# A recurrence and a gated unit on one core: small convolution tiles, a state carried in place in PSUM, and a new loop order

The kernel runs on one core of one Trainium2 chip. The metric is device time in microseconds (us) of that core, lower is better. A run is called slow when it lies over 1.5% above the fastest of its kernel, and ratios use fast runs alone.

## What is computed

```python
# r, k, v: (4, 8, 768, 48); w, u: (8, 48); all float32
for t in range(S):                                   # a state of 48x48 per head
    cur = einsum('bhd,bhe->bhde', u * k[t], v[t])
    y[t] = einsum('bhd,bhde->bhe', r[t], state + cur)
    state = w * state + einsum('bhd,bhe->bhde', k[t], v[t])
x = y.transpose(0, 2, 1, 3).reshape(B, S, 384)
gate = sigmoid(causal depthwise convolution of x, 5 taps)
out = (gate * (x @ w_val)) @ w_out                   # both weights 384x384
```

## The kernel before

The sequence is cut into chunks of 128 positions. Inside a chunk the outputs are masked attention; between chunks a state is carried and decayed. Two chunks make a step (256 positions), so there are 12 steps, three to a batch. Each engine gets its instructions in the order of lists of tokens such as `A:0.1` (attention of the second chunk of a step). Four steps are ordered token by token in a head; eight follow in a loop, over a list called STEP.

The parts that the change touches:

```python
def bonus(n):                                  # u*k*r sums, S
    kv_ps = ps_kv.tile([128, 512], F32)        # the one state bank; step 0: another bank
    st["kv_tile", n, 0] = kv_ps                # state(n, 0) goes into the same bank
    ...                                        # 8 matmuls
def state(n, cl): ...                          # KV: 4 matmuls into kv_ps
def carry(n, cl):                              # ID: adds the decayed state, on TensorE
    nc.tensor.matmul(out=kv_ps, lhsT=ident, rhs=zin, start=False, stop=True)
def decay(n, cl):                              # ZE, on VectorE
    nc.vector.tensor_tensor(out=z, in0=kv_ps, in1=wcm, op=ALU.mult)
def y_out(n, cl):                              # Y: 40 matmuls into 32-row groups:
    ...                                        # 12 for the state, 16 attention, 12 bonus
def conv(n):                                   # C: 64x64 tiles, 4 at once
    g_ps = [ps_mm.tile([128, W + C], F32) for i in range(2)]     # 2 banks of 384 columns
    for T0, t1, tn in [(0, 0, W), (2, 0, 0)]:
        for t in range(KW):
            for q in range(2):
                for i in range(2): ...         # 40 matmuls, 20 of 256 and 20 of 128 columns
LOADS = "r0 k0 r1 k1 v0 r2 k2 Wv v1 Wo r3 v2 k3 r4 ..."          # cut; Wo ahead of r3
STEP = """
    Y:-1.1 YE:-1.1 Y:-1.0 A:0.1 A:0.0 YE:-1.0 CV:0.0 M:0.3 KS:1.0 M:0.2 S:0.0 C:-1.0 V:-1.1
    SG:-1.1 V:-1.0 SE:0.0 RS:1.0 SG:-1.0 M:0.0 DV:0.0 M:0.1 KT:1.0 RT:1.0 HT:-1.1 KV:0.0
    ID:0.0 HT:-1.0 O:-1.0 O:-1.1 ZE:0.0 KV:0.1 KE:1.0 ID:0.1 RE:1.0 ZE:0.1 OE:-1.0 OE:-1.1
    PR:1.0
"""
# A attention, M mask, S bonus, C convolution, SG sigmoid, V value, HT gate*value, O project,
# KT/RT transposes of k and r, KE/RE/YE/OE evacuations, PR product k*r, KS/RS scalings
```

Of the kernel before, what the change touches and what calls it, by code (L numbers as in the profile page):

```python
# [8 lines left out]
F32 = mybir.dt.float32  # L9
# [7 lines left out]
def kernel(  # L17
# [165 lines left out]

    wv_st = consts.tile([128, NT, DM], F32)
    wo_st = consts.tile([128, NT, DM], F32)

    wval = consts.tile([128, NT, 4, 128], BF16)
    wout = consts.tile([128, 4, DM], BF16)
    cw5b = consts.tile([KW, DM], BF16)
    cwT = consts.tile([128, NT, KW], F32)  # L190
    cwd = consts.tile([128, NT, KW, 64], BF16)
    id64 = consts.tile([128, 64], BF16)

    def prep_conv():
        nc.vector.tensor_copy(cw5b, cw5)
        cw_ps = ps_tr.tile([128, NT, 8], BF16, name="tr_ps")
        for T in range(NT):
            nc.tensor.transpose(
                cw_ps[:, T, 0:KW], cw5b[:, T * 128 : T * 128 + 128], ident[0:KW, 0:KW]
            )  # L200
        nc.vector.tensor_copy(cwT, cw_ps[:, :, 0:KW])
        for q in range(2):
            rows = slice(64 * q, 64 * q + 64)
            nc.vector.tensor_copy(id64[rows], ident[rows, rows])
        nc.vector.tensor_tensor(
            out=cwd.rearrange("p t k x -> p (t k) x"),
            in0=id64[:, None, :].to_broadcast([128, NT * KW, 64]),
            in1=cwT.rearrange("p t k -> p (t k)")[:, :, None].to_broadcast([128, NT * KW, 64]),
            op=ALU.mult,
        )  # L210

    def cast_wval():
        wv = wv_st.rearrange("p k (t x) -> p k t x", x=128)
        nc.gpsimd.tensor_copy(wval[:, :, 0::2, :], wv[:, :, 0::2, :])
        nc.gpsimd.tensor_copy(wval[:, :, 1::2, 64:128], wv[:, :, 1:3, 0:64])
        nc.gpsimd.tensor_copy(wval[:, :, 1::2, 0:64], wv[:, :, 1:3, 64:128])

    def cast_wout(part):
        if part:
            nc.scalar.copy(out=wout[64:128, 1::2, :], in_=wo_st[0:64, 1:3, :])  # L220
            nc.scalar.copy(out=wout[0:64, 1::2, :], in_=wo_st[64:128, 1:3, :])
        else:
            nc.gpsimd.tensor_copy(wout[:, 0::2, :], wo_st[:, 0::2, :])
# [83 lines left out]
    def bonus(n):  # L307
        if n == 0:
            kv_ps = ps_mm.tile([128, 512], F32, name="mm_ps")
        else:  # L310
            kv_ps = ps_kv.tile([128, 512], F32, name="kv_ps")
            st["kv_tile", n, 0] = kv_ps
        s_ps = kv_ps[:, DM : DM + U * H].rearrange("p (c h) -> p c h", c=U)
        pr = st["pr", n]
        for cl in range(U):
            for p in range(NP):
                nc.tensor.matmul(  # L317
                    out=s_ps[:, cl, 2 * p : 2 * p + 2],
                    lhsT=pr[:, p, cl * C : cl * C + C],
                    rhs=uw2[:, p, :],  # L320
                    start=(cl == 0 and p == 0),
                    stop=(cl == U - 1 and p == NP - 1),
                    skip_group_check=True,
                )
        st["s_ps", n] = s_ps
# [41 lines left out]
    def state(n, cl, idle=0):  # L367
# [7 lines left out]
        for p in range(NP):  # L375
# [5 lines left out]
                stop=(c == 0 and p == NP - 1),  # L381
# [4 lines left out]
    def carry(n, cl):  # L386
        nc.tensor.matmul(  # L387
            out=st["kv_ps", n, cl].rearrange("p n a d -> p (n a d)"),
            lhsT=ident,
            rhs=st["zin", n, cl].rearrange("p n a d -> p (n a d)"),  # L390
            start=False,
            stop=True,
            skip_group_check=True,
        )
# [52 lines left out]
    def conv(n, idle=0):  # L447
        b, cu = divmod(n, NU)
        xT, t0 = xT_t[b % 2], cu * W
        g_ps = [ps_mm.tile([128, W + C], F32, name="mm_ps") for i in range(2)]  # L450
        warm(g_ps[0][:, 0:C], idle)
        parts = [(0, 0, W), (2, 0, 0)]
        if n == N - 1:
            parts = [(0, 0, C), (0, C, C), (2, 0, 0)]
        for T0, t1, tn in parts:
            for t in range(KW):
                for q in range(2):
                    for i in range(2):
                        T = 2 if T0 else i
                        c0, n0, o0 = (i * C, C, W) if T0 else (t1, tn, t1)  # L460
                        rows = slice(64 * q, 64 * q + 64)
                        qo = (q + i) % 2
                        nc.tensor.matmul(  # L463
                            out=g_ps[i][64 * qo : 64 * qo + 64, o0 : o0 + n0],
                            lhsT=cwd[rows, T, t, :],
                            rhs=xT[rows, T, t0 + c0 + t : t0 + c0 + t + n0],
                            start=(t == 0 and T0 == 0 and t1 == 0),
                            stop=(t == KW - 1),
                            skip_group_check=True,
                        )  # L470
        st["g_ps", n] = g_ps

    def gate_at(n, i):
        if ("gate", n) not in st:
            st["gate", n] = ffn.tile([128, 2, W + C], BF16, name="gate")
        nc.scalar.activation(out=st["gate", n][:, i], in_=st["g_ps", n][i], func=AF.Sigmoid)  # L476

    def value(n, i, idle=0):
        b, cu = divmod(n, NU)
        xT, t0 = xT_t[b % 2], PAD + cu * W  # L480
        v_ps = ps_at.tile([128, NP, 128], F32, name="at_ps")
        v_ps = v_ps.rearrange("p n x -> p (n x)")[:, 0 : W + C]
        warm(v_ps[:, 0:C], idle)
        for kt in range(NT):
            nc.tensor.matmul(  # L485
                out=v_ps[:, 0:W],
                lhsT=wval[:, kt, i, :],
                rhs=xT[:, kt, t0 : t0 + W],
                start=(kt == 0),
                stop=(kt == NT - 1),  # L490
                skip_group_check=True,
            )
        for kt in range(NT):
            nc.tensor.matmul(  # L494
                out=v_ps[:, W : W + C],
                lhsT=wval[:, kt, 2 + i, :],
                rhs=xT[:, kt, t0 + i * C : t0 + i * C + C],
                start=False,
                stop=(kt == NT - 1),
                skip_group_check=True,  # L500
            )
        st["v_ps", n, i] = v_ps

    def gated(n, i):
        if ("hT", n) not in st:
            st["hT", n] = ffn.tile([128, 2, W + C], BF16, name="hT")
        nc.vector.tensor_tensor(  # L507
            out=st["hT", n][:, i], in0=st["v_ps", n, i], in1=st["gate", n][:, i], op=ALU.mult
        )

    def project(n, cl, idle=0):
# [4 lines left out]
        parts = [(0, cl * C, 0), (1, cl * C, 1)]  # L516
        parts.insert(1 + cl, (cl, W, 2 + cl))
        for j, (i, c0, k) in enumerate(parts):
            nc.tensor.matmul(  # L519
                out=o_ps,  # L520
                lhsT=hT[:, i, c0 : c0 + C],
                rhs=wout[:, k, :],
                start=(j == 0),
                stop=(j == 2),
# [19 lines left out]
    def ok(n):  # L544
# [6 lines left out]
        r0 k0 r1 k1 v0 r2 k2 Wv v1 Wo r3 v2 k3 r4 k4 v3 v4 k5 r5 k6 v5 r6 v6 k7 r7 k8 v7 r8 k9 v8  # L551
# [3 lines left out]
        RS:1.0 A:0.0 A:0.1 KS:1.0 PR:0.0 RS:2.0 S:0.0 M:0.2 KT:1.0 M:0.3 M:0.0 M:0.1 KS:2.0 CV:0.0  # L555
        SE:0.0 KV:0.0~4 KE:1.0 RT:1.0 ZE:0.0 RE:1.0 WV:0.0 KV:0.1 DVD:0.0 A:1.1~9 RT:2.0 M:1.3
        ID:0.1 Y:0.1 Y:0.0 PR:1.0 RE:2.0 ZE:0.1 M:1.2 KT:2.0 A:1.0 S:1.0 YE:0.1 M:1.0 YE:0.0 C:0.0
        M:1.1 KE:2.0 PR:2.0 SE:1.0 CV:1.0 A:2.1 KV:1.0~4 SG:0.0 ID:1.0 M:2.3 ZE:1.0 V:0.1 SG:0.1
        V:0.0 KV:1.1 DV:1.0 ID:1.1 M:2.2 ZE:1.1 RS:3.0 WO:0.0 Y:1.1 YE:1.1 WP:0.0 Y:1.0 KS:3.0
        S:2.0 HT:0.1 A:2.0 YE:1.0 M:2.0 SE:2.0 RT:3.0 CV:2.0 C:1.0 HT:0.0 RE:3.0 V:1.1 KV:2.0  # L560
        SG:1.0 ID:2.0 O:0.0 DVD:2.0 SG:1.1 OE:0.0 M:2.1 ZE:2.0 V:1.0 HT:1.1 Y:2.0 YE:2.0 KT:3.0
        KE:3.0 O:0.1 Y:2.1 HT:1.0 PR:3.0 A:3.1 M:3.3 YE:2.1 OE:0.1 TL:0.0 S:3.0 M:3.2 C:2.0 SG:2.0
        A:3.0 V:2.1 M:3.0 V:2.0 SG:2.1 O:1.1 KS:4.0 M:3.1 SE:3.0 CV:3.0 HT:2.0 HT:2.1 O:1.0 OE:1.1
        OE:1.0 KT:4.0 KV:3.0 KE:4.0 RS:4.0 RT:4.0 RE:4.0 O:2.1 O:2.0 ZE:3.0 KV:3.1 ID:3.1 OE:2.1
        OE:2.0 ZE:3.1 DV:3.0 PR:4.0
    """
    STEP = """
        Y:-1.1 YE:-1.1 Y:-1.0 A:0.1 A:0.0 YE:-1.0 CV:0.0 M:0.3 KS:1.0 M:0.2 S:0.0 C:-1.0 V:-1.1
        SG:-1.1 V:-1.0 SE:0.0 RS:1.0 SG:-1.0 M:0.0 DV:0.0 M:0.1 KT:1.0 RT:1.0 HT:-1.1 KV:0.0
        ID:0.0 HT:-1.0 O:-1.0 O:-1.1 ZE:0.0 KV:0.1 KE:1.0 ID:0.1 RE:1.0 ZE:0.1 OE:-1.0 OE:-1.1  # L570
        PR:1.0
    """
    TAIL = """
        Y:11.1 Y:11.0 YE:11.1 YE:11.0 C:11.0 V:11.1 SG:11.1 HT:11.1 V:11.0 SG:11.0 HT:11.0 O:11.1
        O:11.0 OE:11.1 OE:11.0
# [7 lines left out]
    def issue():  # L583

        while loads:
            x = loads[0]
            if x == "Wv":
                nc.sync.dma_start(out=wv_st, in_=moe_w_val.rearrange("(t p) n -> p t n", p=128))
            elif x == "Wo":
                nc.sync.dma_start(out=wo_st, in_=moe_w_out.rearrange("(t p) n -> p t n", p=128))  # L590
# [118 lines left out]
```

## Time and profile before

| | before |
|---|---|
| time, median of 4 runs beside the changed kernel | 105.85 us (104.90 to 107.17) |
| profiled execution, span | 101.8 us |
| TensorE instructions, weight loads counted | 4548 |
| first bonus of the loop (starts the fifth step) | 41.45 us |
| from there to the last bonus, 7 periods | 46.55 us |
| from the last bonus to the end | 13.81 us |

The page of the kernel before gives these lines: busy time with its share and number of instructions by engine, the queue of the instruction fetch (packets, MB, share), and the shares of the chain that ended last (the work followed back from the last instruction, at each step to what released it).

```profile
PE 90.7 (89%) x2266; PEld 74.4 (73%) x2266; DVE 69.4 (68%) x136; ACT 73.4 (72%) x121; POOL 63.4 (62%) x63
...
q8 instruction: 17, 0.28, 1.1%
...
PE 57%; SPq 13%; DMA 10%; ACT 5%; DVE 5%; POOL 4%; issue 3%; ACTq 0%; POOLq 0%; DVEq 0%
```

TensorE holds the chain for 57% of the span. "issue", time in which the engine on the chain waits for nothing that the profile shows, is 3%.

### The profile page before, as it was taken

How to read it: one execution, taken by the hardware profiler on the slowest of the kernel's cores; microseconds unless marked ns; L12 is line 12 of the kernel's file. 1: busy time of each engine (PE TensorE's matmuls, PEld its weight loads, DVE VectorE, ACT ScalarE, POOL GpSimd, SP SyncE). 2: the span in 40 equal slices, each digit the busy share in tenths (PEclk: the TensorE clock that was granted, in tenths of full speed). 3: DMA queues.
4: the chain of work that ended last, by engine and by line, in shares of the span. 5: the costliest groups of instructions: out<-in, count | busy, mean ns of one | idle time of the engine just before them, and what ended most of it. 6: DMA issues, size and time to landing. Idle time of an engine off the chain costs nothing.

```text
span 101.8 us, 5137 instructions
## 1 busy us (share of the span) xinstructions
PE 90.7 (89%) x2266; PEld 74.4 (73%) x2266; DVE 69.4 (68%) x136; ACT 73.4 (72%) x121; POOL 63.4 (62%) x63
## 2 busy tenths in 40 slices
PE   4998499989698899999899999999999999978840
PEld 4696297878576787888778878889788797956710
DVE  4395867898781785985956969769488595890210
ACT  5088165999885999879579598794987958836430
POOL 7927949834847949797694894966949850050000
PEclk9999999999999999999999999999999999999999
DMA  0999999597999999979897969899897999910304
GB/s 5 215 230 226 226 239 291 134 332 129 213 229 188 203 214 222 199 183 175 170 244 139 250 126 225 177 184 261 149 216 174 357 368 361 371 65 26 135 0 155
DMA packets 67345, 20.38 MB, mean 200 GB/s; under 512 B 63478, under 2 KB 67324, under 8 KB 67324
## 3 DMA queue, kind: packets, MB, share of 16 engines
q1 hardware_dynamic: 66492, 20.07, 85.3%
q8 instruction: 17, 0.28, 1.1%
q10 hardware_dynamic: 832, 0.00, 0.5%
q14 instruction: 4, 0.03, 0.1%
HBM read 15.35 MB, written 4.72 MB: 197 GB/s over the span
## 4 chain that ended last, share of the span: by engine, by line
PE 57%; SPq 13%; DMA 10%; ACT 5%; DVE 5%; POOL 4%; issue 3%; ACTq 0%; POOLq 0%; DVEq 0%
DMA r_st<-in_r_dram 10%; PE mm_ps L463 10%; PE at_ps L519 10%; PE mm_ps L412 9%; PE at_ps L485 7%; SPq L71 7%; PE tr_ps L283 4%; PE at_ps L347 4%; PE at_ps L244 4%; SPq L590 4%; PE at_ps L494 3%; PE kv_ps L376 2%; PE kv_ps L317 2%; ACT kT L292 2%; DVE at L360 2%
## 5 line engine op out<-in xcount | busy, mean ns | idle before, releaser
L360 DVE TENSOR_TENSOR at<-at_ps,mask 128x512 bf16<-128x512 f32 x48 | 30.9, 683 | 5.4 <-PE at_ps L347 5.4
L332 POOL TENSOR_TENSOR dv<-v_st,s_sb 128x768 bf16<-128x768 f32 x10 | 14.8, 1477 | 17.4 <-DVE s_sb L329 17.4
L230 POOL TENSOR_TENSOR rs<-r_st,dr 128x768 bf16<-128x768 f32 x11 | 20.1, 1829 | 4.4 <-DMA r_st<-in_r_dram 4.3
L259 POOL TENSOR_TENSOR ks<-k_st,dk 128x768 bf16<-128x768 f32 x11 | 20.7, 1886 | 2.7 <-PE kv_ps L387 1.8
L252 ACT COPY rT<-at_ps 128x1024 bf16<-128x1024 bf16 (+1 forms) x13 | 15.9, 1234 | 3.0 <-PE at_ps L244 3.0
L399 DVE TENSOR_TENSOR z<-kv_ps,wcm 128x384 bf16<-128x384 f32 x20 | 11.1, 556 | 9.8 <-PE kv_ps L387 8.1
L292 ACT COPY kT<-tr_ps 128x1024 bf16<-128x1024 bf16 x11 | 11.2, 1015 | 5.9 <-PE tr_ps L283 5.9
L507 DVE TENSOR_TENSOR hT<-at_ps,gate 128x384 bf16<-128x384 f32 x24 | 12.3, 548 | 4.3 <-PE at_ps L494 4.3
L519 PE MATMUL at_ps<-wout,hT 128*128 128x384 bf16 x72 | 13.9, 326 | 1.5 <-DVE hT L507 1.4
L476 ACT ACTIVATE gate<-mm_ps 128x384 bf16<-128x384 f32 x24 | 10.5, 489 | 5.7 <-PE mm_ps L463 5.2
L532 ACT COPY o_sb<-at_ps 128x384 f32<-128x384 f32 x24 | 10.8, 495 | 4.0 <-PE at_ps L519 4.0
L463 PE MATMUL mm_ps<-xT,cwd 64*64 64x256 bf16 (+1 forms) x500 | 12.6, 242 | 0.9 <-ACT xT L444 0.6
L485 PE MATMUL at_ps<-xT,wval 128*128 128x256 bf16 x72 | 11.9, 274 | 0.0
L268 ACT CAST vb<-v_st 128x768 bf16<-128x768 f32 x12 | 10.3, 859 | 2.2 <-DMA v_st<-in_v_dram 2.2
L444 ACT CAST xT<-mm_ps 128x384 bf16<-128x384 f32 x24 | 11.1, 507 | 1.1 <-PE mm_ps L412 0.9
L463 PEld LDWEIGHTS <-cwd 64*64 64x64 bf16 x500 | 10.7, 106 | 1.4 <-issue 1.0
L519 PEld LDWEIGHTS <-hT 128*128 128x128 bf16 x72 | 6.6, 98 | 5.4 <-DVE hT L507 1.9
L300 DVE TENSOR_TENSOR pr<-tr_ps,rT 128x1024 bf16<-128x1024 bf16 x11 | 7.5, 683 | 4.1 <-ACT kT L292 2.1
L412 PE MATMUL mm_ps<-at,vb 128*32 128x128 bf16 x384 | 9.5, 219 | 0.0
L347 PE MATMUL at_ps<-rT,kT 48*128 48x128 bf16 x192 | 8.8, 228 | 0.5 <-ACT kT L292 0.4
L244 PE MATMUL at_ps<-ident,rs 128*128 128x128 bf16 x96 | 8.2, 235 | 0.9 <-POOL rs L230 0.9
L283 PE MATMUL tr_ps<-ident,ks 128*128 128x128 bf16 x88 | 7.1, 228 | 1.7 <-POOL ks L259 1.7
(79 smaller groups left out, 142.9 us busy)
## 6 DMA issues: line engine op xcount, KB each, us to landing
r_st<-in_r_dram SPq DMA_DIRECT2D x12, 384.0 KB, 5.2
k_st<-in_k_dram SPq DMA_DIRECT2D x24, 192.0 KB, 4.6
v_st<-in_v_dram SPq DMA_DIRECT2D x24, 192.0 KB, 4.9
out_dram<-o_sb SPq DMA_DIRECT2D x11, 384.0 KB, 5.1
wv_st<-in_moe_w_val_dram SPq DMA_DIRECT2D x1, 576.0 KB
wo_st<-in_moe_w_out_dram SPq DMA_DIRECT2D x1, 576.0 KB, 7.3
out_dram<-o_sb SPq DMA_DIRECT2D x2, 192.0 KB, 1.9
wt<-in_w_dram ACTq DMA_DIRECT2D x2, 0.8 KB, 2.5
```

Source lines behind the costliest of these rows:

```text
L230: eng.tensor_tensor(out=rs_t[n % 2][:, :, ps[0] : ps[1], :, 0:D].rearrange("p s n a d -> p (n a) s d"), in0=r_st[n][:, hs], in1=dr[:, hs], ...
L252: nc.scalar.copy(out=st["rT", n][:, ps[0] : ps[1], :].rearrange("x n (i s) -> x s n i", s=2), in_=st["r_tr", n, ps[0]],)
L259: eng.tensor_tensor(out=ks_t[n % 3][:, cs, :, :, 0:D].rearrange("p c n a d -> p c (n a) d"), in0=k_st[n][:, cs], in1=dk[:, None, :, :].to_ ...
L292: nc.scalar.copy(out=st["kT", n].rearrange("x n (c i) -> x c n i", c=U)[:, cls[0] : cls[1]], in_=tr)
L332: eng.tensor_tensor(out=dv_t[n % 2].rearrange("p c (h d) -> p (c h) d", d=D), in0=v_st[n].rearrange("p c h d -> p (c h) d"), in1=st["s", n ...
L347: nc.tensor.matmul(out=at_ps[par][:, p, :], lhsT=kT[rows, p, cs], rhs=rT[rows, p, cs], start=(p == 0), stop=(p == NP - 1), skip_group_chec ...
L360: nc.vector.tensor_tensor(out=st["at", n, cl][:, par], in0=st["at_ps", n, cl][par], in1=mask[:, None, :].to_broadcast([128, NP, 128]), op= ...
L412: nc.tensor.matmul(out=y_ps[32 * q : 32 * q + 32, T, :], lhsT=lt, rhs=rh, start=q not in first, stop=last, skip_group_check=True,)
L463: nc.tensor.matmul(out=g_ps[i][64 * qo : 64 * qo + 64, o0 : o0 + n0], lhsT=cwd[rows, T, t, :], rhs=xT[rows, T, t0 + c0 + t : t0 + c0 + t + ...
L485: nc.tensor.matmul(out=v_ps[:, 0:W], lhsT=wval[:, kt, i, :], rhs=xT[:, kt, t0 : t0 + W], start=(kt == 0), stop=(kt == NT - 1), skip_group_ ...
L507: nc.vector.tensor_tensor(out=st["hT", n][:, i], in0=st["v_ps", n, i], in1=st["gate", n][:, i], op=ALU.mult)
L519: nc.tensor.matmul(out=o_ps, lhsT=hT[:, i, c0 : c0 + C], rhs=wout[:, k, :], start=(j == 0), stop=(j == 2),)
```

## The change

The intent: take work off TensorE, which bounds the loop. The convolution goes into 32x32 tiles, twelve at once, with a third gate bank; the carry becomes an add on VectorE, in place in PSUM; and all orders (loads, head, loop, tail) were searched anew with a model of the queues. The diff, cut to its core:

```diff
+    PLACE = (lambda q: q, lambda q: q ^ 2, lambda q: q ^ 1)
     def carry(n, cl):
-        nc.tensor.matmul(out=kv_ps, lhsT=ident, rhs=zin, start=False, stop=True, ...)
+        nc.vector.tensor_tensor(out=kv_ps, in0=kv_ps, in1=st["zin", n, cl], op=ALU.add)
     def conv(n):
-        g_ps = [ps_mm.tile([128, W + C], F32, name="mm_ps") for i in range(2)]
-        ...                                        (40 matmuls in 64x64 tiles)
+        g_ps = [ps_mm.tile([128, W], F32, name="mm_ps") for T in range(2)]
+        g_ps.append(ps_at.tile([128, W], F32, name="at_ps"))
+        for t in range(KW):
+            for T in range(NT):
+                for q in range(4):
+                    rows = slice(32 * q, 32 * q + 32)
+                    o = 32 * PLACE[T](q)
+                    nc.tensor.matmul(out=g_ps[T][o : o + 32, :], lhsT=cwd[rows, T, t, :],
+                                     rhs=xT[rows, T, t0 + t : t0 + t + W], ...)
     def value(n, i):                               (6 matmuls of 256 and 6 of 128 columns)
+        ...                                        (9 of 256: two tiles, then one)
+    def load_wo(): ...                             (Wo in 7 loads, rows permuted by PLACE)
     LOADS
-        r0 k0 r1 k1 v0 r2 k2 Wv v1 Wo r3 v2 k3 r4 k4 v3 ...
+        r0 k0 k1 v0 r1 Wv r2 k2 v1 r3 v2 k3 Wo r4 v3 k4 k5 ...
     STEP
-        Y:-1.1 YE:-1.1 Y:-1.0 A:0.1 A:0.0 YE:-1.0 CV:0.0 M:0.3 KS:1.0 M:0.2 S:0.0 C:-1.0 ...
+        Y:-1.1 A:0.0 Y:-1.0 M:0.0 M:0.1 S:0.0 YE:-1.1 YE:-1.0 A:0.1 C:-1.0 V:-1.0 M:0.2 SE:0.0
+        RS:1.0 M:0.3 CV:0.0 SG:-1.1 RT:1.0 SG:-1.0 HT:-1.0 V:-1.1 SG:-1.2 KV:0.0 HT:-1.1 KT:1.0
+        O:-1.0 DV:0.0 ID:0.0 ZE:0.0 RE:1.0 O:-1.1 KE:1.0 PR:1.0 OE:-1.1 KV:0.1 ID:0.1 KS:2.0
+        OE:-1.0 ZE:0.1
     HEAD, TAIL: new orders (cut)
```

## The prediction

> **What bounds the kernel now.** I read the page's busy shares first: no engine stands out alone. Then the windows, cut where a step of the main loop begins (the first matmul of `y_out`, L412). Twelve steps of 256 positions make up the kernel; eight of them, from 39.9 us to 92.6 us, are the loop, four are a hand-ordered head. The eight take 52.7 us, 6.585 us each. Columns: window, its length, then busy time and count of PE, PE weight loads, DVE, ACT, POOL, then clock, DMA share and GB/s.
>
> ```profile
> 59.99:66.53 6.54, 6.54 (x183) 5.53 (x186) 5.20 (x10) 5.38 (x10) 5.24 (x4) 1.00 0.93 195
> 79.70:86.28 6.58, 6.58 (x182) 5.55 (x185) 5.21 (x10) 5.23 (x10) 2.72 (x2) 1.00 1.04 363
> ```
>
> PE is busy for the whole of both windows and DVE idles 1.3 us in each. A full PE could still be a waiting one, so I read the chain that ended last, in order of time (start, us, what). Between 46 and 54 us it never leaves PE:
>
> ```profile
> 46.44 1.23 PE mm_ps L412 x80
> 47.67 0.55 PE at_ps L347 x16
> 48.22 0.28 PE kv_ps L317 x8
> 55.43 0.95 PE mm_ps L463 x40
> 56.39 0.43 PE at_ps L485 x3
> 52.07 0.16 PE kv_ps L387
> 52.23 0.97 PE at_ps L519 x6
> ```
>
> So in the loop TensorE is the bound, piece after piece: y 1.23, attention 0.55, bonus 0.28, convolution 0.95, value 1.10 (0.43+0.17+0.33+0.17), two transposes 0.45 each, project 0.97, state twice 0.17, carry twice 0.16; together 6.6. The head is different. Its last wait in the timeline is this one:
>
> ```profile
> 29.43 1.83 POOL L259 TENSOR_TENSOR ks<-k_st,dk 128x768 bf16<-128x768 f32 x1 [1.82 <-PE kv_ps L387]
> 31.31 0.62 PE L283 MATMUL tr_ps<-ident,ks 128*128 128x128 bf16 x8 [0.26 <-POOL ks L259]
> 33.07 0.69 DVE L300 TENSOR_TENSOR pr<-tr_ps,rT 128x1024 bf16<-128x1024 bf16 x1 [2.09 <-ACT kT L292]
> ```
>
> The releaser shown is a matmul that this scaling does not need in that way; k of step 3 was issued from 22.0 to 25.3 us and such loads land 4.6 us later, that is up to 29.9, so I take the wait for that load. Until there the head runs at the speed of the loads (DMA share 0.92 to 1.03 in every window up to 33 us). After 33.8 us PE has hardly a gap.
>
> **What the Trainium skill says.** "TensorEngine Tiling (Array Packing)", section Key Properties: tiles work independently of each other, while a change of tiling mode drains the array. The trace agrees with both. The convolution's 0.95 us is 0.09 and five rounds of 0.11 (256 columns, a third of value's 0.33) and five of 0.056 (128 columns, an eighth of the transposes' 0.45), so its four tiles run together and issuing is not its limit. The 0.09 is the change of mode: the last of eight bonus matmuls, 0.025 us apart from 61.54, starts near 61.73, and the first convolution matmul at 61.83. "TensorE: Matmul & The Clock Gate", section Part 3 (Packing small matmuls), gives a further tile about 4 ns, so twelve tiles cost hardly more than four. "VectorE: DVE Perf Modes", sections on the perf-mode tiers and the DRAIN: tensor_tensor with a PSUM operand runs at one element a cycle, and a read of what the same engine just wrote needs a semaphore. Agreed for the first, by the groups (busy us, mean ns, then idle before):
>
> ```profile
> L360 DVE TENSOR_TENSOR at<-at_ps,mask 128x512 bf16<-128x512 f32 x48 | 30.9, 683 | 5.4 <-PE at_ps L347 5.4
> L399 DVE TENSOR_TENSOR z<-kv_ps,wcm 128x384 bf16<-128x384 f32 x20 | 11.1, 556 | 9.8 <-PE kv_ps L387 8.1
> ```
>
> No run has the second yet. "PSUM — Partial Sum Buffer", section PSUM bank collisions: two engines may not read one bank at once. So the product `pr` may not read the transposed k while ScalarE evacuates it; the 2.09 us wait above shows that order.
>
> **The change, part by part.** *Convolution.* Before: 20 matmuls of 256 columns and 20 of 128, on 4 tiles, 0.95. After: 60 of 256 on 12 of 16 tiles, 5 rounds of 0.11 us plus the drain of 0.09, 0.65: saves 0.30. *Value:* nine matmuls of 0.109 instead of six of 256 and six of 128 columns: 0.98, saves 0.12. *Carry:* 16 in all, 1.33 a step, 0.16 each: saves 0.21 a step. *Order:* the attention of one half now stands between the two y halves and the other after the bonus, so two more mode changes, 2 x 0.09 lost. TensorE's floor goes from 6.6 to about 6.6-0.30-0.12-0.21+0.18 = 6.1.
>
> *VectorE.* The adds into PSUM: 16 of 128x384 at 556 ns, 1.33 a step, 0.74. The gating product becomes one of 512 and one of 256 columns, 683 + about 415 (an estimate from the 1.0 ns a column between 384 and 512): as before. Busy goes from 5.1 to about 5.85 a step, 0.95 of a 6.1 us step. *ScalarE:* three gates of 256 columns, about 0.36 each (0.49 less 128 columns), for two of 0.49: +0.1. Both stay below the floor as sums. What decides is their order.
>
> *The new circle.* Bonus and state share the one state bank. The bonus of a step must wait for the last decay of the step before, and that decay now stands on VectorE behind the product and the add. In time from the end of that decay: bonus 0.06 to 0.28, attention to 0.58 (with drains), convolution from 0.71 (its third bank waits for a mask) to 1.30, value of two tiles to 2.04, r transposes to 2.49, r evacuation (1.32, overlapping its follower by 0.1) from 2.74, k evacuation 3.97 to 5.0, product 5.05 to 5.73, add to 6.25, wait for its own semaphore, decay to 6.87. VectorE's four masks, gating and first add and decay lead to 4.9 by themselves, so no gap is left there either. The built program has each of these waits. Two of three steps close this circle (6.8 to 6.9); the third has no second state and is bound by TensorE at about 6.45. Mean 6.7. My evacuation latencies (0.25) are rounded up, and the mean of what I could shave is 0.1, so I take 6.6 a step: the loop gains nothing, although TensorE has 0.5 us less to do.
>
> *Head.* The output weights (0.59 MB) go behind k of step 3, whose load had 11 loads of 0.39 MB and 1.18 MB of weights in front of or in it, and now has 0.59 MB less. At the 220 to 300 GB/s of that stretch, 2.0 to 2.7 us sooner. v of step 0 comes earlier too, so the work ahead of it can start sooner. I count 1.9. *Tail:* the last convolution 1.04 to 0.65, its gate chain a little longer: -0.2. Sum: 105.6 - 1.9 - 0.2 + 8 x 0.015 = 103.6.
>
> **Rivals.** *(1) TensorE stays the bound.* For it: 6.1 against 6.585, and the order was searched for. Against it: the circle. It would give 105.6 - 3.9 - 2.1 = 99.6; with some stalls 101. *(2) The circle costs its full 6.75 or more and the head gives back little,* because ScalarE and VectorE were as full as PE there (6.59 us of ACT in the 6.90 us to 39.9). It would give 105.6 + 1.3 - 0.5, about 106.5. *(3) Transfers:* the loop's loads arrive at 1.18 MB in about 6.1 us (share 0.93 of 6.54), so a 6.1 us step would meet that. But the last load is issued at 73.4 us, and its step begins at 86, so eight microseconds of lead stand between: I leave it out. *(4) Twelve tiles do not run together* and 60 pairs issue at the 15 ns of y_out (1.23/80): 0.9, no gain in the convolution, circle 7.1: 107.
>
> **Range and chances.** Between rivals 1 and 2 my sum lies in the middle, with 0.2 us a step of doubt (1.6 us) and 1.2 in the head. That is some 2 us: 101.2 to 106.6. Faster needs under 103.5, so it is near even, and I lean neither way: 0.46 faster, 0.44 same, 0.10 slower.
>
> **What would show it.** Convolution pieces of 0.6 to 0.7 us right for tiling; 0.9 wrong. DVE busy over 5.7 in a loop window, with PE under 6.3 of it, right for the circle; a chain that in the loop passes through kT, pr, kv_ps add and z, and PE waiting ahead of the bonus for z, right. PE full again at 6.1 a step: rival 1. The k scaling of step 3 starting near 27 us, right for the head; at 29 wrong. An add far from 0.56 us, or steps over 6.8, would break the sum.

## The result, and the profile after

The changed kernel takes 110.44 us (110.31 to 112.64, four runs) against 105.85. The ratio is 1.046, 95% interval 1.036 to 1.056: slower, and outside the predicted range. (A ratio is the mean time of one kernel's fast runs over that of the other's of the same rounds, so it is not quite the ratio of the medians.)

The same lines of the page, after:

```profile
PE 91.5 (84%) x2448; PEld 68.5 (63%) x2448; DVE 77.0 (71%) x153; ACT 72.7 (67%) x131; POOL 64.4 (59%) x66
...
q8 instruction: 19, 0.31, 1.2%
...
PE 30%; SPq 21%; DVE 16%; ACT 14%; issue 10%; DMA 7%; DVEq 0%; ACTq 0%
```

TensorE no longer holds the chain, as intended: 57% became 30%. But "issue" went from 3% to 10% of a longer span, over 7 us more. Cut at the bonus starts:

| us | before | after | difference | predicted |
|---|---|---|---|---|
| start to first bonus of the loop | 41.45 | 45.56 | +4.1 | -1.9 |
| 7 loop periods | 46.55 | 49.07 | +2.5 | +0.1 |
| last bonus to the end | 13.81 | 14.03 | +0.2 | -0.2 |
| span | 101.8 | 108.7 | +6.9 | |

(The profiled execution of before, 103.95 us, was faster than all four timed runs of it beside the change, so the profiles differ by more than the medians.)

**The pieces came out nearly as predicted.** These are groups of the changed kernel by shape (busy us, mean ns of one, then idle before with its releaser):

```profile
L405 DVE TENSOR_TENSOR kv_ps<-kv_ps,z 128x384 f32<-128x384 f32 x16 | 8.9, 556 | 0.8 <-PE kv_ps L393 0.8
...
L505 DVE TENSOR_TENSOR hT<-at_ps,gate 128x512 bf16<-128x512 f32 x12 | 8.2, 685 | 4.2 <-PE at_ps L491 4.1
```

The add takes 556 ns. The convolution takes 0.56 us from its first to its last start where nothing stops it, 60 matmuls, against 0.81 for 40 before; the twelve tiles do run together, as the matmuls of its first round start 3 to 4 ns apart (67.19 to 67.23 us). From its first start to the first of the next piece it is 0.76 us against 0.96, so it saves 0.20 us a step of the 0.30 predicted.

**The loop without its stops.** The chain through one undisturbed step of the changed kernel (start, us, what) is the circle of the prediction, from one bonus to the decay ahead of the next:

```profile
66.58 0.35 PE kv_ps L334 x8
...
68.02 0.76 PE at_ps L491 x6
68.78 0.46 PE at_ps L264 x8
...
69.26 1.03 ACT rT L272
...
70.43 1.02 ACT kT L312
...
72.09 0.57 DVE kv_ps L405
...
72.68 0.56 DVE z L410
```

The next bonus starts at 73.29: 6.71 us for a step with two states. The next, with one, takes 6.30. Three windows from bonus to bonus in the changed kernel, and one of the kernel before (window, its length, then busy time and count of PE, PE weight loads, DVE, ACT, POOL, then clock, DMA share, GB/s):

```profile
66.58:73.29 6.71, 6.64 (x203) 5.10 (x204) 6.24 (x13) 5.17 (x11) 4.76 (x3) 1.00 1.00 209
73.29:79.59 6.30, 6.24 (x199) 4.87 (x200) 5.73 (x11) 5.46 (x10) 4.62 (x4) 1.00 0.88 191
79.59:87.92 8.33, 6.44 (x200) 5.02 (x192) 5.44 (x12) 5.90 (x12) 5.71 (x4) 1.00 1.11 356
```

```profile
61.54:68.24 6.70, 6.70 (x192) 5.69 (x189) 5.20 (x11) 5.54 (x11) 5.09 (x4) 1.00 0.94 198
```

So an undisturbed two-state step is as long as before, 6.71 against 6.70, though TensorE's pieces are shorter. The prediction said just that. (One of its signs failed: PE was to be busy for under 6.3 us, and the profile counts 6.64 of 6.71.) The third window is what it did not say.

**The stops.** In the chain of the changed kernel, inside the window of 8.33 us:

```profile
81.06 0.65 PE at_ps L491 x5
81.71 1.42 issue
83.13 0.27 PE at_ps L491
```

Five of six value matmuls run, then TensorE stands for 1.42 us with nothing to wait for. I numbered TensorE's instructions in the order of the program, weight loads counted, and laid the trace over them. The sixth matmul is number 3775, and number 3777 is 193 above a multiple of 256. Counted from 0, every gap marked "issue" of TensorE that I followed, in every kernel of this study, lies one or two instructions ahead of such a number, 193 + 256 k. The packets of the page's q8 line, the instruction fetch, are 16 KB each (0.31 MB in 19), and there are 17 of them for the 4548 instructions of before and 19 for 4905: one for about 256 instructions. In the traces such a packet takes 0.9 to 2.1 us, and where TensorE stops it goes on 1.2 to 1.7 us after the packet's end. Over all 20 profiles, laid over their programs in the same way: of 341 crossings of such a border (449 paired with the first packet, 705 with the second, and so on) none came sooner than 1.19 us after the packet's end. So TensorE goes on only when the next block has come. What starts a packet, no record shows.

Counting gaps over 0.2 us between the starts of two matmuls at these borders, between first and last bonus of the loop: 0.76 us before (two), 2.99 us after (three, of 0.45, 0.85 and 1.69). Less its stops, a loop period is 6.54 us before and 6.58 after. So in this pair of profiles 2.2 us of the loop's 2.5 are stops.

The larger of the two stops before, at number 1984, stands in the stretch from 46 to 54 us that the prediction read as never leaving PE. Its list of lines took the convolution of the next step instead of this one:

```profile
48.51 0.90 PE mm_ps L463 x36
49.40 0.26 issue
49.66 0.25 PE mm_ps L463 x4
```

**The head.** The prediction said that the k scaling of step 3 would start near 27 us, and it does: 27.30 us, against 29.43 before.

```profile
27.30 1.81 POOL L279 TENSOR_TENSOR ks<-k_st,dk 128x768 bf16<-128x768 f32 x1 [1.66 <-DMA k_st<-in_k_dram]
```

Yet the loop starts 4.1 us later. The chain of the changed kernel there:

```profile
28.20 3.21 DMA wo_st<-in_moe_w_out_dram
...
31.51 0.13 ACT wout L241
...
32.25 0.93 ACT gate L481 x3
33.18 0.91 ACT kT L312
```

The output weights, now loaded behind k of step 3, land at 31.4 us. ScalarE, in order, waited 3.75 us for them, with three sigmoids and the k evacuation of step 3 behind. And this execution's granted clock was 0.5 to 0.7 from 32.6 to 40.8 us, right after TensorE had stood still: six project matmuls took 1.92 us there, 0.97 elsewhere. I count about 2 us for that (projects 0.95, r transposes 0.4, convolution 0.5, others 0.2).

### The profile page after: what moved, and what is told of

Same layout as the page of the kernel before. It is cut to its first block, busy times and chain, and to the rows that moved or that the text cites.

```text
span 108.7 us, 5534 instructions
## 1 busy us (share of the span) xinstructions
PE 91.5 (84%) x2448; PEld 68.5 (63%) x2448; DVE 77.0 (71%) x153; ACT 72.7 (67%) x131; POOL 64.4 (59%) x66
## 4 chain that ended last, share of the span: by engine, by line
PE 30%; SPq 21%; DVE 16%; ACT 14%; issue 10%; DMA 7%; DVEq 0%; ACTq 0%
SPq L71 14%; PE mm_ps L468 6%; ACT kT L312 6%; PE at_ps L491 5%; PE at_ps L518 5%; ACT rT L272 4%; DVE at L377 4%; PE mm_ps L423 4%; DVE kv_ps L405 4%; DVE z L410 4%; PE at_ps L364 4%; DMA r_st<-in_r_dram 4%; DVE hT L505 3%; DMA wo_st<-in_moe_w_out_dram 3%; PE at_ps L264 3%
## 5 line engine op out<-in xcount | busy, mean ns | idle before, releaser
L349 POOL TENSOR_TENSOR dv<-v_st,s_sb 128x768 bf16<-128x768 f32 x11 | 16.2, 1477 | 24.7 <-PE at_ps L468 15.5
L505 DVE TENSOR_TENSOR hT<-at_ps,gate 128x512 bf16<-128x512 f32 (+1 forms) x24 | 13.1, 553 | 9.9 <-PE at_ps L491 6.1
L518 PE MATMUL at_ps<-wout,hT 128*128 128x384 bf16 x72 | 15.0, 343 | 2.9 <-ACT wout L241 1.7
L491 PE MATMUL at_ps<-xT,wval 128*128 128x256 bf16 x108 | 15.5, 273 | 1.4 <-issue 1.4
L468 PE MATMUL mm_ps<-xT,cwd 32*32 32x256 bf16 x480 | 10.9, 283 | 1.8 <-issue 1.3
L481 ACT ACTIVATE gate<-mm_ps 128x256 bf16<-128x256 f32 x24 | 8.2, 383 | 5.3 <-PE at_ps L468 4.6
L364 PE MATMUL at_ps<-rT,kT 48*128 48x128 bf16 x192 | 10.1, 222 | 2.1 <-ACT kT L312 0.9
L468 PE MATMUL at_ps<-xT,cwd 32*32 32x256 bf16 x240 | 10.6, 283 | 0.0
L468 PEld LDWEIGHTS <-cwd 32*32 32x32 bf16 x720 | 7.4, 89 | 5.0 <-issue 3.1
L491 PEld LDWEIGHTS <-wval 128*128 128x128 bf16 x108 | 9.2, 97 | 1.9 <-issue 0.2
```

The lines of the kernel that those rows point to most:

```text
L349: eng.tensor_tensor(out=dv_t[n % 2].rearrange("p c (h d) -> p (c h) d", d=D), in0=v_st[n].rearrange("p c h d -> p (c h) d"), in1=st["s", n ...
L468: nc.tensor.matmul(out=g_ps[T][o : o + 32, :], lhsT=cwd[rows, T, t, :], rhs=xT[rows, T, t0 + t : t0 + t + W], start=(t == 0), stop=(t == K ...
L491: nc.tensor.matmul(out=v_ps[:, j], lhsT=wval[:, kt, T, :], rhs=xT[:, kt, t0 : t0 + W], start=(j == 0 and kt == 0), stop=(kt == NT - 1), sk ...
L505: nc.vector.tensor_tensor(out=st["hT", n][:, Ts], in0=st["v_ps", n, i][:, 0 : 2 - i], in1=st["gate", n][:, Ts], op=ALU.mult,)
L518: nc.tensor.matmul(out=o_ps, lhsT=hT[:, T, cl * C : cl * C + C], rhs=wout[:, T, :], start=(T == 0), stop=(T == NT - 1),)
```

## The experiments

All outputs are right. The table has what the profiles show; first bonus, stops (in the loop) and period (loop less its stops, by 7) as defined above. A profile is one execution, and the stops differ from one to the next, so times are judged by the timed runs. Profiles that fell in a slow run are marked s; I use them for the places of the stops, not for differences. Only the change, after_again, spread and both are classed as clearly slower than before; the record calls the other comparisons unclear. They ran on several chips, each beside its own runs of before. The single run before_again, beside the other runs of before on its chip (103.34 to 109.06 us), would count as slow.

| run | instructions | median us | ratio to before | first bonus | stops | period |
|---|---|---|---|---|---|---|
| before | 4548 | 105.85 | | 41.45 | 0.76 | 6.54 |
| before_again | 4548 | 107.01 (one) | | 42.27 | 3.07 | 6.53 |
| the change | 4905 | 110.44 | 1.046 | 45.56 | 2.99 | 6.58 |
| after_again | 4905 | 110.58 | 1.044 | 43.78 s | 5.71 s | 6.73 s |
| wo_early | 4905 | 109.74 | 1.044 | 44.35 | 2.75 | 6.56 |
| wo_late | 4905 | 108.21 | 1.021 | 42.06 | 2.20 | 6.59 |
| head_before | 4876 | 112.43 | 1.077 | 44.58 | 5.22 | 6.76 |
| order_before | 4883 | 118.66 | 1.134 | 45.31 | 2.93 | 7.85 |
| bonus_bank | 4907 | 113.37 | 1.086 | 42.68 | 0.40 | 7.68 |
| carry_pe | 4937 | 110.85 | 1.053 | 42.91 | 1.81 | 6.81 |
| bonus_tr | 4905 | 109.32 | 1.039 | 42.28 | 2.08 | 6.56 |
| both | 4937 | 110.59 | 1.037 | 42.46 s | 5.20 s | 6.95 s |
| shift112 | 5017 | 109.14 | 1.036 | 42.88 | 4.92 | 6.42 |
| spread | 4905 | 110.41 | 1.048 | 44.48 s | 1.43 s | 7.05 s |
| conv64 | 4185 | 108.50 | 1.031 | 42.60 | 0.32 | 7.06 |
| y_wide | 4313 | 115.72 | none given | 43.21 | none | 7.78 |
| dv_first_late | 4473 | 108.21 | none given | 43.05 | 1.31 | 6.61 |

Theory: the loop is a circle that is no shorter than before; the stops at block borders (every 256 instructions) lengthen it; ScalarE's wait for the output weights delays the head. Rivals are named in the expectations.

### Is the profile typical?

**after_again** and **before_again** are the two kernels once more.

> The changed kernel itself once more, on the chip of the next three, for its spread: 109.5 to 111.5 us, stops at instructions 1729, 2497, 3777 and 4545 again. If the dip of the granted clock around 33 to 41 us was of that one execution, it is elsewhere or gone and the first bonus of the loop comes at 42.3 to 43; if it belongs to this order of work, it is there again and the first bonus is at 45 to 46.

> The kernel before once more with a profile, for its granted clock: if the dips seen in most profiles of the changed kernels also fall on the kernel before, there is a stretch of some slices under 0.9 in this profile or none by chance; if they belong to the new order alone, none. Time 104 to 107.

The borders are the same, with 2241 added (1.66 us), and the stops are larger. The dip of the clock came at another place, and one fell on the kernel before too (0.6 and 0.5 between 10 and 18 us). So dips belong to neither order. They also do not make the difference: one timed run of the change had a granted clock of 1.000 and took 110.31 us, one of before had 1.000 and took 103.73. (The first bonus of after_again, 43.78 us, lies between the two ranges expected.) Stops are not fixed either: the kernel before had 3.07 us in its second profile, and its loop then took 48.79 us, only 0.3 less than the change's 49.07. So one pair of profiles does not settle how many microseconds of stops the change adds.

### The head

**wo_early** puts Wo back ahead of r3 in the loads.

```diff
-r0 k0 k1 v0 r1 Wv r2 k2 v1 r3 v2 k3 Wo r4 v3 k4 k5 ...
+r0 k0 k1 v0 r1 Wv r2 k2 v1 Wo r3 v2 k3 r4 v3 k4 k5 ...
```

> Changed kernel with one thing back as it was: the output weights are loaded ahead of r of step 3 again. Theory H (head): the slower head comes from ScalarE, which casts the output weights in order and sat 3.7 us on their load, with everything behind it; expected: that wait is gone, the first bonus of the loop (45.56 us in the changed kernel, 41.51 before) comes at 41 to 42, the dip of the granted clock at 33 to 41 us is gone, time 106 to 107. Rival: the head is slow because of its new order of tokens; then the first bonus stays near 45 and the time near 110.

The wait on Wo was gone, but the wait moved: GpSimd's scaling of r waited 4.8 us for its load and ScalarE's cast of v 4.7 us for its own. First bonus at 44.35, no gain, in a profile whose clock was at 0.5 from 25.6 to 32.4 us. The expectation was missed.

**head_before** takes LOADS and HEAD from the kernel before (with a third sigmoid in each step).

> The changed kernel with the orders of loads and of the head (everything ahead of the loop) as they were before, the loop's order and all other parts as changed. Head theory (the new head is what starts the loop late): the first bonus of the loop at 41.5 to 42.5 us instead of 45.6, and the time 107 to 108. Rival (the head costs what it costs because of the parts, the third gate bank and the split loads): first bonus after 43.5 and the time 109 to 110.5. The block borders fall elsewhere, which moves stops by about 1 us either way.

Missed too: first bonus at 44.58, 112.43 us. The clock was at 0.5 from 11 to 18 us, but order_before below has the same head, no such dip ahead of its loop, and 45.31. The old head does not fit the new parts, so the new head as such is not at fault. (This execution also had stops of 2.73 and 1.52 us in the loop.)

**wo_late** leaves the loads and moves the cast of Wo and the projection that needs it.

```diff
-... V:0.1 DVD:2.0 WO:0.0 C:1.0 ... V:1.0 O:0.1 KE:3.0 Y:2.0 PR:3.0 Y:2.1 YE:2.0
+... V:0.1 DVD:2.0 C:1.0 ... V:1.0 KE:3.0 Y:2.0 PR:3.0 Y:2.1 WO:0.0 O:0.1 YE:2.0
```

> The changed kernel with the cast of the output weights on ScalarE (and the one projection that needs it at once) moved later in the head, behind the evacuation of the fourth step's k; the loads and the loop are untouched. Head theory (ScalarE, held up by the output weights that land at 30 to 31.5 us because seven small loads in a row take SyncE's queue 4.5 us, delays the sigmoids and evacuations behind it): no wait on the output weights over 1 us, first bonus of the loop at 40.5 to 41.8, time 1 to 2 us under the changed kernel's. Rival (the head is bound by the loads behind, r and k of the fourth and fifth step): first bonus stays at 42.3 to 43, time unchanged.

No wait on Wo is left, and the time falls by 2.2% against after_again on the same chip (means of the two fast runs of each, 107.24 and 109.67). The first bonus, 42.06 us, just misses the 41.8 expected. From 20 us on the chain has no load in it; between 30 and 34 us, for one, it is TensorE's own work:

```profile
30.88 0.66 PE at_ps L491 x6
31.53 1.23 PE mm_ps L423 x80
32.76 0.59 PE at_ps L518 x3
```

So the wait is gone, and behind it stands the engines' own work: no kernel with the new parts started its loop before 42.06 us. How much of the 2.4 us is the head is not shown. The wait stands in the other kernels with the old place of the cast too, as in bonus_tr:

```profile
30.02 0.83 ACT L241 CAST wout<-wo_st 128x768 bf16<-128x768 f32 x1 [2.69 <-DMA wo_st<-in_moe_w_out_dram]
```

It is 1.0 us in carry_pe, 2.2 in conv64 and shift112, 2.7 in bonus_tr and 3.75 in the change, and the first bonus comes at 42.91, 42.60, 42.88, 42.28 and 45.56. In the first four the clock was full from 16 us up to the loop, and carry_pe's chain from 20 us on has no load in it either. So a wait of up to 2.7 us hardly delays the loop. Of the change's 45.56, the longer wait and the clock dip share the rest; no run separates them.

### The circle

**order_before**: the new parts, all orders as before.

> Small tiles, third gate bank and in-place carry on VectorE as changed, but loads, head, loop and tail in the order of before: the parts without the new order. If the new order is at fault: first bonus of the loop at 41.5 to 42.5 us, undisturbed steps at or under 6.6 us, and the time 103.5 to 106. If the parts themselves are at fault (VectorE's adds on the state's path, or stops at block borders, which the smaller tiles bring in any order): steps of 6.7 to 7.1 us and 107 to 110.

Periods of 7.85 us. VectorE's add stands in line ahead of other work and waits for TensorE's state, 8.2 us in the window from 45 to 100 us (waited for, times, longest):

```profile
DVE kv_ps L405 <- PE kv_ps L393: 8.2, 9, 1.0
```

The gating product stands behind the add, and TensorE's projection waited 6.3 us for that product. The new order is not the fault; without it the parts lose 1.3 us a period. (In the kernel before, VectorE's decay waited 6.1 us for the same state in the loop at no such loss, so the wait by itself is not the sign; what stands behind it is.)

**bonus_bank** and **bonus_tr** move bonus out of the state's bank, into the convolution's pool and into the bank of the k transposes:

```diff
-        kv_ps = ps_kv.tile([128, 512], F32, name="kv_ps")
-        st["kv_tile", n, 0] = kv_ps
+        kv_ps = ps_tr.tile([128, 512], F32, name="tr_ps")        # bonus_bank: ps_mm, "mm_ps"
```

> Changed kernel with the bonus in a bank of the y and gate pool, not in the state bank, so that it needs no decay of the step before. Theory C (circle): the loop's period of 6.71 us in steps with a second state is the circle bonus, convolution, value, r and k evacuation, product, add, decay; cut, undisturbed steps fall to 6.1 to 6.35 and the time by 2 to 3 us to about 108. Rival D: VectorE's own length (four masks, gating, two adds, two decays, product) sets 6.7; then the period stays above 6.6 and the time within 0.8 us of 110.4.

> The changed kernel, but the bonus sums go to the bank of the k transposes instead of the state's bank, so that bonus no longer waits for the decay of the state before; unlike bonus_bank, no other bank changes hands. Circle theory (bonus to state to add to decay to bonus sets an undisturbed step at 6.71 us): undisturbed two-state steps fall to 6.1 to 6.45 us, the wait of bonus for the decay is gone, and the time falls by 1.5 to 2.5 us to 108 to 109. Rival (VectorE's or TensorE's length sets the step): undisturbed two-state steps stay at 6.6 to 6.75 us and the time at 110 to 111.

bonus_bank tells nothing of the circle, as it made a new wait, of the convolution's bank for the bonus evacuation, in the window from 42 to 92 us:

```profile
PE mm_ps L467 <- DVE s_sb L345: 7.2, 7, 1.5
```

bonus_tr did take the wait away, with no other of TensorE in its place, and its period is 6.56. The circle through the shared bank is cut, and on average the step is not shorter: the rival, "another length sets the step", was right on that. The single steps differ: two two-state steps, less their stop, come to 6.1 and 6.2 us, as the circle theory had it, while two without a stop take 7.31 and 7.11. The time, 109.32 us, lies between the two expected. The chain of bonus_tr leads through VectorE's own queue, its masks behind its decay:

```profile
61.70 0.57 DVE kv_ps L404
62.27 0.02 issue
62.29 0.56 DVE z L409
62.85 1.79 DVE at L376 x3
64.64 0.09 DVE s_sb L345
```

**carry_pe** puts the carry back on TensorE; **both** is carry_pe and bonus_tr.

```diff
-        nc.vector.tensor_tensor(out=kv_ps, in0=kv_ps, in1=st["zin", n, cl], op=ALU.add)
+        nc.tensor.matmul(out=kv_ps, lhsT=ident, rhs=zin, start=False, stop=True, ...)
```

> Changed kernel with the carry undone: the old state is added by a matmul with the identity again, all else as changed. Theory C: one add (0.57 us) less on the circle, a matmul (0.16 us and about 0.25 to VectorE) instead of it: undisturbed two-state steps 6.71 to about 6.35 to 6.45, time about 1.5 to 2 us less, 108.5 to 109. Rival D: two adds less on VectorE, 1.1 us a step: a period of 6.2 and 2.5 to 3 us less. Rival F (TensorE's instruction stops alone matter): no change beyond 0.5 us.

> bonus_tr and carry_pe in one: bonus in the bank of the k transposes and the carry as a matmul on TensorE. If in bonus_tr VectorE's own length took the place of the circle (it is 0.56 us longer per step by the add), then with both gone the undisturbed two-state steps are TensorE's length, 6.2 to 6.45 us, and the stops at block borders grow or stay. If another wait binds, undisturbed steps stay at 6.6 to 6.75.

Neither is shorter on average. In carry_pe one two-state step fell to 6.37 us, as the circle foretold, but others were 7.02 and 7.71 with no stop in them, and the one-state steps 6.60 (6.30 in the change). With both, the steps without a stop were 6.57, 6.60 (a one-state step) and 7.02 us, where TensorE's length had been put at 6.2 to 6.45. What holds these I did not find. That bank, VectorE and TensorE nearly tie, so that taking one away shows the next, would fit but is not shown.

### The stops

**shift112** adds 56 idle matmuls in gaps of the head, so that each block border falls 112 instructions earlier in the work.

```diff
-A:0.1 A:0.0 ... Y:0.1~6  ... KV:0.1   ... KV:1.0   ... Y:1.0~2
+A:0.1~16 A:0.0 ... Y:0.1~22 ... KV:0.1~8 ... KV:1.0~8 ... Y:1.0~10
```

> Changed kernel with 56 idle matmuls more in gaps of the head (112 instructions of PE). Theory F: the stops of PE inside the convolution (0.36, 0.85, 1.69, 0.76 us at about 46.6, 59.8, 81.4 and 95.7 us) are where PE's instruction number is 193 above a multiple of 256, a border of blocks fetched 16 KB at a time, reached too soon after a dense run. Moved by 112, stops must be at number 1473, 2241 and 3009 (60th, 35th and 29th pair of a convolution), none at the former places; one at 3777 (11th pair) small or none; sum about 2 us instead of 3.3; time 0.5 to 1.5 us less. Rival S: the stops are waits for a semaphore of the loop's own order; then they stay at the same matmuls of the same steps.

The stops moved with the borders. The first convolution after the loop's second bonus ran through in 0.56 us in the changed kernel (from 53.32 us). In shift112 number 2241 lies in it, and it stops there:

```profile
50.76 0.05 PE at_ps L468
50.81 0.90 issue
51.71 0.28 PE at_ps L468 x3
```

The place in the instruction stream is thereby shown to be the cause, not the work that stands there. The expected sum of 2 us was missed: there were seven stops, 4.92 us in all, as the loop crosses some 11 borders wherever they lie. Less its stops the period is 6.42, under the 6.59 that the undisturbed steps of the change make on average. So part of a stop can fall where a wait stood anyway, and taking stops off in full then takes off too much.

**spread** moves one projection into the dense run of outputs, attention and convolution, with the number of instructions kept.

```diff
-Y:-1.1 A:0.0 Y:-1.0 M:0.0 M:0.1 S:0.0 ...  RE:1.0 O:-1.1 KE:1.0 PR:1.0 OE:-1.1
+Y:-1.1 A:0.0 Y:-1.0 M:0.0 M:0.1 O:-2.1 S:0.0 ...  RE:1.0 KE:1.0 PR:1.0
```

> The changed kernel with one of the two projections of each step moved into the next step, between the second output and bonus, so that TensorE's dense run of 328 instructions is broken by 0.97 us of work in 12 instructions; the number of instructions is the same and the block borders in the program lie within 12 instructions of where they were. Fetch theory: the stops at the borders in the loop fall from 2.5 to 3 us in all to under 1, and the time falls by 1 to 2.5 us, unless the later projection lengthens the circle. Rival (the stops come with the positions in the program, not with the density ahead of them): stops of the same sum at the same borders.

The stops stayed at the borders 2497 and 3777, with a small one at 3265, 1.43 us in all, and the later projection lengthened the period to 7.05: no gain. The profile fell in a slow run, so the smaller sum says little. Inconclusive on density.

**conv64** takes only the small tiles back: 30 matmuls of 256 columns in 64x64 tiles, third bank and orders kept.

```diff
-                for q in range(4):
-                    rows = slice(32 * q, 32 * q + 32)
-                    o = 32 * PLACE[T](q)
+                for q in range(2):
+                    rows = slice(64 * q, 64 * q + 64)
+                    o = 64 * (q ^ (T == 1))
```

> The changed kernel with the convolution back in 64x64 tiles: 30 matmuls of 256 columns instead of 60, 4185 TensorE instructions instead of 4905. Fetch theory (the dense run of attention, output and convolution goes through 256 instructions faster than the next block is fetched): the dense run falls from 328 to 268 instructions and lasts 0.25 us longer; stops at block borders in the loop fall from some 2.9 us in all to under 1.5, and the time falls to 108 to 109.5. Rival (TensorE's work sets the loop, which is what the smaller tiles were for): each step 0.25 us longer, so 112 to 113.

The convolution lasts 1.02 us instead of 0.56, and the undisturbed two-state step 7.18 instead of 6.71: the convolution is on the path to its full 0.46 us. And the stops are nearly gone, 0.32 us in all with 720 instructions fewer. In the profiled loops the small tiles thus save 3.4 us (seven periods of 6.58 instead of 7.06) and give 2.7 of them back at the borders. The timed runs do not tell the two kernels apart: 108.50 us, with an interval of 0.988 to 1.074 of before. Nor is this the convolution of before, which is faster: up to the next piece it takes 1.22 us here, 0.96 before and 0.76 in the change. Against before the small tiles save 0.20 us a step, 1.4 us in the loop, less than the 2.2 us of further stops in the profiles of the change and of before.

That a lower pace alone does not remove the stops shows in order_before: with the full number of instructions (398 from bonus to bonus) in periods of 7.85 us it still stopped for 2.93 us, conv64 with 337 in 7.06 for 0.32.

**y_wide** keeps the small tiles and does the output sums in fewer, wider matmuls (27 for 40). y_wide_late adds wo_late; all_three adds both; before_wide is the kernel before with the same edit.

```diff
-            for G in range(3 * NP):
-                mm(G, zf[:, 32 * G : 32 * G + 32], rT[:, G // 3, ...])
+            for G, wide in ((0, 2), (2, 1), (3, 1), (4, 2), (6, 2), (8, 1), (9, 1), (10, 2)):
+                mm(G, zf[:, 32 * G : 32 * G + 32 * wide], rT[:, G // 3, ...], wide=wide)
-        for G in range(3 * NP):
-            mm(G, dv[:, cl, 32 * G : 32 * G + 32], ident, last=True)
+        for T in range(NT):
+            mm(4 * T, dv[:, cl, 128 * T : 128 * T + 128], ident, last=True, wide=4)
```

> The changed kernel with the same output sums in fewer and wider matmuls: 8 instead of 12 for the state's part, 3 instead of 12 for the bonus part, in the same number of rounds of the array, so TensorE's time stays and its instructions fall from 4905 to 4313. Fetch theory (TensorE stops at borders of blocks of 256 instructions where it goes through a block faster than the next one comes): the stops in the loop fall from 3 us or more to under 1, the steps without stops stay at 6.71 and 6.30 us, and the time falls by 2 to 3 us to 107.5 to 108.8. Rival (the stops belong to the small tiles of the convolution or to the third gate bank, not to the number of instructions): stops as before, time within 0.7 us of the changed kernel's.

> y_wide and wo_late in one. If the two losses, the head's and the stops', are separate, their gains add: first bonus of the loop at 41 to 42 us, few stops, 105 to 106.5, within 1% of the kernel before. If one hides the other: 107 to 108.5.

> y_wide, wo_late, and both (bonus in the bank of the k transposes and the carry on TensorE). If only the stops kept the loop of both from TensorE's own length, its undisturbed steps are now 6.2 to 6.4 us and the time is 102.5 to 104.5, faster than both kernels. If another wait binds there, steps of 6.55 to 6.75 and 105 to 106.5.

> The kernel before with the wider output matmuls alone: 3956 TensorE instructions instead of 4548. Its stops are few (about 1 us in the loop), so by the fetch theory it gains at most that: 104.3 to 105.5. If fewer instructions shorten TensorE's work in itself, it gains more, 0.1 us or more per step: 103.5 to 104.5.

The stops vanished: none at a border in any of the four. y_wide's steps repeat to 0.01 us: 8.17, 7.89, 7.08, 8.17, 7.89, 7.08, 8.17. But all four were far slower (115.72, 115.05, 121.05 and 117.84 us), and the expected times were missed by 7 to 17 us. My edit alternates widths, and each change of width costs: in the timeline of y_wide (start, us, line, idle), eight state matmuls last 0.92 us, where the twelve of 32 columns were part of an output of 0.67.

```profile
64.05 0.92 PE L423 MATMUL mm_ps<-rT,z 128*64 128x128 bf16 x8
64.90 0.41 PE L423 MATMUL mm_ps<-at,vb 128*32 128x128 bf16 x16
65.24 0.34 PE L423 MATMUL mm_ps<-ident,dv 128*128 128x128 bf16 x3
```

From a matmul of one width to the next of another it is 0.15 to 0.17 us from start to start; between rounds of one width it is 0.056. Six changes an output at about 0.1 us more, and two outputs a step, make 1.2 us by this estimate, where two of three steps lost 1.5 and 1.6 us and the third, with the state's part in one output alone, 0.4.

**dv_first_late** is wo_late with only the bonus part made wide (3 matmuls for 12), and first, so that the width changes once.

```diff
+        for T in range(NT):
+            mm(4 * T, dv[:, cl, 128 * T : 128 * T + 128], ident, wide=4)
         z = st.get(("zin", n, cl))
-        for G in range(3 * NP):
-            mm(G, dv[:, cl, 32 * G : 32 * G + 32], ident, last=True)
```

> wo_late with the bonus part of each output done first and in 3 matmuls over the full array instead of last and in 12 of 32 columns; the state's part stays in 32-column tiles, so that the width changes once per output (y_wide changed it six times, at 0.16 us each, which took 1.5 us per step). 4473 TensorE instructions instead of 4905. Fetch theory: stops in the loop under 1.5 us in all instead of about 3; each step 0.1 to 0.2 us longer by the change of width ahead of the outputs; time 106.5 to 108, at or a little under wo_late. Rival (stops are not lessened by fewer instructions in the dense run): 109 or more.

Stops of 1.31 us and the shortest loop of all changed kernels, 47.60 us, but the median is 108.21 us, as for wo_late, with runs from 106.00 to 109.43 (slow ones among them). The fast runs have means of 106.63 us here (two) and 104.07 for before (three), 1.025 with no interval. The best of the changed kernels do not beat the kernel before.

## Why the prediction was wrong

By its own steps:

1. **TensorE bounds the loop before:** the chain says so, stop aside, and no run tested it by itself. The new parts in the old order were slower, on VectorE's side.
2. **TensorE's savings: right in kind.** The convolution with what leads to the next piece fell from 0.96 to 0.76 us (0.95 to 0.65 predicted). conv64 shows that its length is on the path in full: 0.46 us of convolution, 0.47 of step.
3. **VectorE's costs: right.** Add 556 ns (556), the gating product 685 and 422 (683 and 415).
4. **The circle: right in length, partly wrong in reason.** Undisturbed steps of 6.71 and 6.30 us (6.8 to 6.9 and 6.45 written, 6.6 taken for the mean; 6.58 measured less stops), along the very path foretold. But bonus_tr and both show that the shared bank is not the bound: without it the step is on average as long. What the bound is stays open.
5. **The head, -1.9 us: the step that failed, and the largest term.** The load of k did come 2.1 us sooner. That the loop would start sooner with it was the error. With the clock full from 16 us on, the new head started the loop at 42.28 to 42.91 us, and with the cast of the weights out of the way (wo_late, with a dip from 20.0 to 23.4 us) at 42.06, with no load in the chain from 20 us on: the engines' own work holds the start, above the 41.45 of before. In the profiled execution (45.56) two things came on top: ScalarE, in order, waited 3.75 us for the output weights that had moved behind k, and a clock dip added some 2 us, which fell elsewhere in other profiles, of before too. wo_late is 2.2% faster, two fast runs against two; how much of that is the wait stays open.
6. **The stops at block borders: missing.** The prediction counted busy time and waits, and passed over an "issue" in the chain that it read. 2.2 us of the 2.5 us by which the profiled loop grew are stops. That they follow the borders is shown (shift112), and that kernels with fewer instructions have next to none (conv64, y_wide). That the instruction fetch is what TensorE waits for rests on the packets' times: no border was crossed within 1.19 us of the end of its packet. How many microseconds of the median they cost is not settled: they vary from 0.8 to 3.1 us between executions of before, 3.0 to 5.7 of after, and no run removed them at no other cost.
7. **The tail, -0.2:** +0.2, with a stop of 0.76 us in it.

Rival 2 (circle at full length, head gives little, 106.5) came nearest in kind; it too lacked the stops. The sum is thus a loop that gains nothing, some 2 us more of stops in it by one pair of profiles, and a head later by about 1 us instead of earlier by 1.9. That is less than the 4.6 us between the medians; the rest is not accounted for.

## What to carry to other kernels

When a profile says "issue" for an engine with thousands of instructions, number them and see whether the gaps recur every 256; then instructions are a cost of their own, and a change that trades few long matmuls for many short ones pays there. A transfer that lands sooner helps only if nothing else holds the work behind it, and if what it passed in the queue is not wanted by an in-order engine in between: look for the consumer of the one that was moved back. And where several engines are nearly full, lightening one may gain nothing; test it by cutting the supposed circle before searching for an order.

## What the Trainium skill lacked or had wrong

- "Runtime: NRT & Kernel Launch", section Instruction fetch mechanics, gives blocks of 16 KiB (256 instructions), which these runs agree with, and says that the cost of a crossing is mostly hidden. Here TensorE stood 0.2 to 2.7 us at single borders; in the changed kernel 2.99 us in all of a loop of 49 us, at about 60 instructions per us (397 a period of 6.6 us). With 337 a period (conv64) it stopped for 0.3 us in all, with 347 (y_wide) not at all.
- "TensorEngine Tiling (Array Packing)", section Key Properties, says that a change of tiling mode drains TensorE, without a size. Here a change among widths of 32, 64 and 128 columns took 0.15 to 0.17 us from start to start, against 0.056 without (y_wide), and the steps were up to 1.6 us longer.
